# Four half-tile weight loads move from SyncE's DMA queue to ScalarE's, in a one-core attention and two-layer expert kernel

## The chip, the cores and the metric

The kernel runs on one core of a Trainium2 chip. The metric is the device time of one execution in microseconds (us). The time of a kernel is the median of several executions; one further execution was taken by the hardware profiler, and all rows below are from it. The engines are TensorE (PE, with its weight loads as PEld), VectorE (DVE), ScalarE (ACT), GpSimd (POOL) and SyncE (SP), which here only issues DMAs.

## The reference

The computation is a chunked attention followed by two gated feed-forward layers, in float32.

```python
# attention: 4 batches, 8 heads, 768 tokens, head size 64; chunks of 32 queries
# see 8 memory keys, 16 tokens to the left, the chunk, 8 tokens to the right
scores = scale * np.matmul(q_c, k_full.transpose(0, 1, 3, 2))
a = softmax(scores); out[:, :, c_start:c_end] = np.matmul(a, v_full)
# x: 3072 tokens x 512
h = x @ w_in                                    # 512 x 2048
x = h * (1.0 / (1.0 + np.exp(-1.702 * h))) @ w_out    # 2048 x 512
g = x @ w_gate; val = x @ w_val                 # 512 x 1536
y = g * (1.0 / (1.0 + np.exp(-g))) * val @ w_out      # 1536 x 512
```

The weights arrive as float64 words (the inputs that begin with `moe` are viewed as pairs of 32-bit words). The kernel turns each weight tile into float32 itself.

## The kernel before

The 3072 tokens are six blocks of 512, and each block is four groups of 128 tokens. Attention works on a group (g = 0 to 23): PE makes the scores (`scores_first`, L693), DVE subtracts the row maximum (L719, L720), ACT takes the exponential (L725), DVE and ACT sum, guard, invert and weigh (L736, L141, L144, L742), PE transposes the weights (L153), ACT copies them out of PSUM (`keep_e`, L162) and PE multiplies with the values (L169). For the first block ACT then rounds the attention output to the operand `xh` (`hi_x`, L757), keeps a copy (L764), DVE makes the remainder `xl` (L769), and PE starts the first feed-forward layer on `xh` and `xl` (`plain_up`, L542). Later blocks run in a steady order of products (L446) and down products (L581).

A weight tile comes from the array `wr` as 128 partitions of 512 eight-byte words, 512 KB. `load_raw` (L262) loads it into `raw`; three buffers rotate, and four spare tiles of the weight pool serve for tiles 3 to 6. A tile of `w_out` is one DMA (L271). A tile of `w_in` is reordered on the way: it is two DMAs of 256 KB (L276), one for partitions 0 to 63 (a = 0) and one for partitions 64 to 127 (a = 1), each of 256 pieces of 1 KB. Then ACT reads both halves in one instruction (`take_words`, L283), DVE shifts and joins the bits (L291, L296), ACT rounds to the high part of the weight (L250), and POOL or DVE makes the low part (L253).

The first tiles in load order are 0, 1, 4, 5, 2, 3, 6, 7 of `wr` (`AT`, L260); load positions 0 to 3 are all in-weights, so each is two halves.

The opening, up to some 57 us, is written out by hand as a list of names in `OPENING` (L951), and each engine runs its instructions in that order, SP's DMA issues among them. `ldw0` to `ldw3` are the loads of positions 0 to 3, `ldk`, `ldq`, `ldv` those of keys, queries and values of a group. On ACT's side, `ex` is the exponential, `ra` the guard, `pr` `take_words`, `ec` `keep_e`, `hi` `hi_x`, `wb`, `wv` and `wa` the high parts of weights, `xf` the copy. On DVE's side, `mx` is the maximum and its subtraction, `sm` the sum, `rc` and `wg` the inverse and the weighing, `cs` and `ct` the shift and the join. On PE's side, `sc`, `te`, `pv` and `ua` are scores, transposes, values and the first feed-forward products. The stretches of the list around the four loads are:

```python
z0 tb0 ldk0 ldq0 sc0 mx0 ex0 sm0 ra0 ldk1 ldk2 ldq1 ldq2 ldk3 sc1 ldk4 z2 z1 mx1 ex1 sm1 rc0 ldw0 ra1
sc2 mx2 ex2 ldq3 ldq4 wg0 pr0 cs0 sc3 sm2 ra2 rc2 wg2 ldv0 ldw1 ldv1 rc1 wg1 te0 ec0 pv0 te1 mx3 ex3 sm3
te2 pr1 ldv2 ec1 cs1 ct1 ldq5 wb0 ra3 rc3 wg3 ct0 ldv3 sumA0/G ec2 hi0 pv1 hi1 wbl0/G pv2 ldw2 ldw3 ldk5
ldk6 te3 xl0 ldq6 sumB0/G ldw4 wv0 xf0 sc4 hi2 xl2 ec3 wa0 wvl0/V pv3 wal0/G xf2 hi3 ua1 mx4 xl3 ldw5
ex4 ua0 ldv4 sm4 hiB0 loB0/G xl1 ra4 wg4 ...  hiA0 xf1 pr3 cs3 pr2
```

Between engines only true dependences make anyone wait. SP has one more kind of wait: a load waits until the load eight places before it has landed, since eight semaphores rotate over the DMAs.

Of the kernel before, what the change touches and what calls it, by code (L numbers as in the profile page):

```python
# [57 lines left out]
def tile_attention_moe_moe(  # L58
# [8 lines left out]
    nc = tc.nc  # L67
# [194 lines left out]
    def load_raw(upto):  # L262
        while len(raws) < min(upto, NRAW):
            i = len(raws)
            if RB <= i < RB + len(spare_raw):
                raws.append(spare_raw[i - RB])
            else:
                raws.append(rpool.tile([P, 512], I64, tag="raw", name="raw", bufs=RB))
            k = AT[i] if i < len(AT) else i
            if k >= 2 * NF1 or k % 4 > 1:  # L270
                nc.sync.dma_start(out=raws[-1], in_=wr[k])  # L271
                continue
            src = wr[k].rearrange("(e d) (b a n) -> a d b e n", e=2, b=2, a=2)
            for a in range(2):
                dst = raws[-1][64 * a : 64 * a + 64].rearrange("d (b e n) -> d b e n", b=2, e=2)
                nc.sync.dma_start(out=dst, in_=src[a])  # L276

    nraw, bits = [2 * len(AT)], {}

# [21 lines left out]
    def next_weights(out):  # L301

        i = nraw[0]
        load_raw(i + RB)
        nraw[0] += 1
        take_words(i)
        yield 0
        shift_words(i)
        yield 0
        join_words(i)  # L310
        out += [bits.pop(i), raws[i]]
# [557 lines left out]
    def tokens():  # L869
# [8 lines left out]
        "ldk": lambda g: load_kv_first("k", g),  # L878
        "ldv": lambda g: load_kv_first("v", g),
        "ldw": lambda i: load_raw(i + 1),  # L880
        "st": store_x,
        "sc": scores_first,
# [153 lines left out]
    for n, (ph, b, ua, ub) in enumerate(seq):  # L1036
# [6 lines left out]
        for u in range(ua, ub):  # L1043
# [47 lines left out]
            if u == ua and nxt is not None and not attends:  # L1091
                src = {1: xd, 2: yd}[nxt[0]][nxt[1]]
# [55 lines left out]
```

## Time and profile before

| what | value |
|---|---|
| median of 3 runs | 1184.48 us (1182.43 to 1184.59) |
| profiled execution | 1181.78 us, of which the span from first to last instruction is 1180.0 us |
| busy share of the span | PE 97%, PEld 88%, DVE 55%, ACT 48%, POOL 29% |
| DMA | 131.47 MB; mean 111 GB/s; in the first 29.5 us 287 GB/s |
| granted TensorE clock, mean | 0.999 |

Busy time says which engine works, not who holds up whom. The views that answer that are the chain of work that ended last, the list of waits, and the timeline of one engine. The span is 1180.0 us long, so one digit of the page's slices covers 29.5 us; the opening is about two of them. The time from a DMA's issue to its landing is given with each line that issues DMAs.

### The profile page before, as it was taken

What the parts mean: (1) busy time and instruction counts of PE and PEld (TensorE: products, weight loads), DVE (VectorE), ACT (ScalarE), POOL (GpSimd) and SP (SyncE); (2) the same over time, 40 slices, a digit from 0 to 9 for tenths busy, and PEclk for the clock granted to TensorE, in tenths of its full rate; (3) what the DMA queues carried; (4) which work ended last, traced back from release to release, by engine and by line L of the source; (5) the groups of instructions that cost most, each with busy time, mean ns of one, the idle gap of its engine ahead of it and who ended that gap; (6) DMA issues with size and microseconds to landing.
All of it is one profiled execution on the core that took longest, in us unless ns stands there. A gap on an engine that the chain in (4) does not pass through costs nothing.

```text
span 1180.0 us, 22292 instructions
## 1 busy us (share of the span) xinstructions
PE 1146.8 (97%) x8908; PEld 1036.3 (88%) x8908; DVE 651.1 (55%) x1130; ACT 567.9 (48%) x1185; POOL 340.5 (29%) x308
## 2 busy tenths in 40 slices
PE   4799999999999999999999999999999999999998
PEld 3688888888899989999998999999999999999997
DVE  5878756556755444443456555354465554454553
ACT  4876554555565445444355444343455543243342
POOL 2553240203534233221335432021245521021010
PEclk9999999999999999999999999999999999999999
DMA  9889835253362322421333321120225130330302
GB/s 287 269 224 269 202 110 166 86 161 92 107 188 81 126 81 81 143 90 36 120 113 116 99 91 51 58 72 1 97 94 169 36 108 2 107 99 10 108 26 83
DMA packets 62920, 131.47 MB, mean 111 GB/s; under 512 B 5728, under 2 KB 26208, under 8 KB 60512
## 3 DMA queue, kind: packets, MB, share of 16 engines
q1 hardware_dynamic: 62816, 130.05, 35.4%
q8 instruction: 70, 1.15, 0.4%
q14 instruction: 34, 0.28, 0.1%
HBM read 98.57 MB, written 31.46 MB: 110 GB/s over the span
## 4 chain that ended last, share of the span: by engine, by line
PE 89%; DVE 4%; ACT 3%; issue 2%; DMA 1%; POOL 1%; SPq 0%; DVEq 0%; ACTq 0%; POOLq 0%
PE y L581 37%; PE ps_a L446 27%; PE ps_c L446 12%; PE ps_b L446 9%; PE ps_s L196 1%; PE ps_o L169 1%; DMA xd<-xf 1%; PE ps_t L153 1%; PE ps_u L542 1%; PE ps_v L169 1%; DMA q<-in_qg 1%; DVE gs L561 0%; ACT g L547 0%; PE ps_k L706 0%; ACT b L428 0%
## 5 line engine op out<-in xcount | busy, mean ns | idle before, releaser
L446 PEld LDWEIGHTS ps_a<-b,w 128*128 128x128 f32 x2832 | 383.9, 189 | 36.9 <-DVE ps_a L498 4.2
L446 PE MATMUL ps_a<-b,w 128*128 128x256 f32 x2832 | 397.1, 283 | 3.5 <-DVE ps_a L498 2.1
L581 PE MATMUL y<-gs,w 128*128 128x512 f32 x1152 | 298.5, 395 | 2.9 <-DVE e L742 1.7
L581 PE MATMUL y<-w,gs 128*128 128x512 f32 x864 | 247.8, 395 | 0.6 <-DVE gs L561 0.5
L581 PEld LDWEIGHTS y<-gs,w 128*128 128x128 f32 x1152 | 204.2, 189 | 39.1 <-DVE gs L561 2.5
L446 PE MATMUL ps_c<-b,w 128*128 128x256 f32 x1224 | 179.1, 282 | 0.0
L446 PEld LDWEIGHTS ps_c<-b,w 128*128 128x128 f32 x1224 | 167.2, 190 | 8.8
L581 PEld LDWEIGHTS y<-w,gs 128*128 128x128 f32 x864 | 144.2, 190 | 14.4 <-DVE gs L561 1.8
L253 POOL TENSOR_TENSOR w<-wf,w 128x512 fp32r<-128x512 f32 (+1 forms) x66 | 75.9, 1151 | 221.5 <-ACT w L250 199.8
L446 PE MATMUL ps_b<-b,w 128*128 128x256 f32 x900 | 133.8, 285 | 0.4 <-DVE ps_b L483 0.3
L549 ACT ACTIVATE g<-ps_b 128x512 f32<-128x512 f32 x72 | 43.0, 598 | 166.2 <-DVE ps_b L504 166.2
L446 PEld LDWEIGHTS ps_b<-b,w 128*128 128x128 f32 x900 | 119.2, 192 | 3.9 <-issue 1.7
L432 DVE TENSOR_TENSOR b<-xl,b 128x512 fp32r<-128x512 f32 x72 | 64.4, 895 | 80.3 <-ACT b L428 80.1
L498 DVE TENSOR_TENSOR ps_a<-m,ps_a 128x256 f32<-128x256 f32 x115 | 48.9, 425 | 105.4 <-PE ps_a L446 99.2
L488 ACT COPY u<-ps_a 128x256 f32<-128x256 f32 x115 | 42.9, 373 | 106.4 <-PE ps_a L446 106.3
L411 POOL TENSOR_TENSOR xl<-xl,t 128x512 f32<-128x512 f32 x18 | 23.3, 1293 | 231.1 <-DVE t L408 229.8
L561 DVE TENSOR_TENSOR gs<-ps_a,gs 128x512 fp32r<-128x512 f32 x118 | 80.9, 685 | 11.8 <-ACT gs L557 11.5
L483 DVE TENSOR_TENSOR ps_b<-p,ps_b 128x256 f32<-128x256 f32 x115 | 49.2, 428 | 61.3 <-PE ps_b L446 56.7
L557 ACT CAST gs<-ps_a 128x512 fp32r<-128x512 f32 x118 | 69.8, 591 | 23.3 <-DVE ps_a L527 15.6
L527 DVE TENSOR_TENSOR ps_a<-g,ps_a 128x512 f32<-128x512 f32 x72 | 50.0, 694 | 45.7 <-PE ps_a L446 45.2
L504 DVE TENSOR_TENSOR ps_b<-u,ps_c 128x256 f32<-128x256 f32 x102 | 43.6, 427 | 50.1 <-PE ps_c L446 49.8
L479 ACT COPY p<-ps_a 128x256 f32<-128x256 f32 x115 | 43.0, 374 | 58.0 <-PE ps_a L446 54.0
(131 smaller groups left out, 1172.8 us busy)
## 6 DMA issues: line engine op xcount, KB each, us to landing
raw<-in_wr SPq DMA_DIRECT2D x49, 512.0 KB, 3.4
xl<-yd SPq DMA_DIRECT2D x12, 1024.0 KB, 4.8
vm<-in_vg SPq DMA_DIRECT2D x22, 512.0 KB, 4.6
kbd<-in_kg SPq DMA_DIRECT2D x32, 256.0 KB, 4.2
raw<-in_wr SPq DMA_DIRECT2D x30, 256.0 KB, 5.0
yp<-o SPq DMA_DIRECT2D x24, 256.0 KB, 3.0
xl<-xd SPq DMA_DIRECT2D x6, 1024.0 KB, 4.8
base<-yp SPq DMA_DIRECT2D x24, 256.0 KB, 3.4
```

Of the source, the lines that this page charges most:

```text
L253: eng.tensor_sub(w[:, 1, o : o + n], f, w[:, 0, o : o + n].bitcast(F32))
L432: (eng or self.engs[k]).tensor_sub(x[:, 1], self.source(k), x[:, 0].bitcast(F32))
L446: nc.tensor.matmul(ps, w[:, a, o + kc * P : o + kc * P + P], x[:, c, kc, :], start=(start and kc == 0 and (a, c) == PASSES[0]), stop=(kc = ...
L479: nc.scalar.copy(p1, ca[:, :n])
L483: add(cb[:, :n], p1, cb[:, :n])
L498: add(ca[:, n:], m, ca[:, :n])
L504: add(cb[:, n:], u2, cc)
L527: late[0] = [lambda: nc.vector.tensor_mul(ca, t, ca), lambda: gs.append(cast(ca))]
L549: nc.scalar.activation(t, c, AF.Silu)
L557: nc.scalar.copy(x[:, 0], g)
L561: nc.vector.tensor_sub(x[:, 1], g, x[:, 0].bitcast(F32))
L581: nc.tensor.matmul(y, lhs, rhs, start=(first and o == 0 and (a, c) == PASSES[0]), stop=(ends and o == len(gs) - 1 and (a, c) == passes[-1]),)
```

## The change

Of load positions 0 to 3, the half with a = 1 is issued by `nc.scalar.dma_start` in place of `nc.sync.dma_start`. Nothing else in the source differs. The names in `OPENING` stay where they are, so the issue comes on ACT's instruction stream at the place that `ldw0` to `ldw3` have in the list.

```diff
             for a in range(2):
                 dst = raws[-1][64 * a : 64 * a + 64].rearrange("d (b e n) -> d b e n", b=2, e=2)
-                nc.sync.dma_start(out=dst, in_=src[a])
+                (nc.scalar if a and i < 4 else nc.sync).dma_start(out=dst, in_=src[a])
```

## Rows read from the trace of the kernel before

**Rows 1.** The page: engines, the granted clock and GB/s in slices, the DMA queues.

```profile
PE 1146.8 (97%) x8908; PEld 1036.3 (88%) x8908; DVE 651.1 (55%) x1130; ACT 567.9 (48%) x1185; POOL 340.5 (29%) x308
...
q1 hardware_dynamic: 62816, 130.05, 35.4%
```

**Rows 2.** Chain that ended last, 0 to 60 us: start us, us, what.

```profile
16.08 0.44 DVE wf L291
...
31.35 4.37 PE ps_u L542 x18
...
37.07 2.69 issue
...
40.08 4.55 PE ps_u L542 x12
...
57.19 3.00 PE y L581 x12
```

**Rows 3.** ACT's timeline: start us, us, operation, output and input, [idle before, its releaser].

```profile
11.95 0.58 ACT L725 ACTIVATE ps_k<-ps_k 128x512 f32<-128x512 f32 x1 [2.39 <-DVE ps_k L720]
...
15.38 0.66 ACT L283 ACTIVATE wh<-raw 128x512 f32<-128x512 f32 x1
17.14 0.21 ACT L141 ACTIVATE r<-r 128x8 f32<-128x8 f32 x1 [1.09 <-DVE r L736]
18.75 1.18 ACT L162 COPY ebd<-ps_t 64x512 f32<-64x512 f32 x2 [1.40 <-PE ps_t L153]
20.58 0.58 ACT L725 ACTIVATE ps_k<-ps_k 128x512 f32<-128x512 f32 x1 [0.65 <-DVE ps_k L720]
21.83 0.68 ACT L283 ACTIVATE wh<-raw 128x512 f32<-128x512 f32 x1 [0.67 <-DMA raw<-in_wr]
23.04 1.18 ACT L162 COPY w<-ps_t 64x512 f32<-64x512 f32 x2 [0.53 <-PE ps_t L153]
...
30.92 0.65 ACT L757 CAST xh<-ps_v 128x256 fp32r<-128x256 f32 x2
...
34.14 0.67 ACT L283 ACTIVATE wh<-w 128x512 f32<-128x512 f32 x1
```

**Rows 4.** SP's timeline: half-tile issues in pairs, the sixth query load, the fifth value load.

```profile
4.82 1.65 SPq L276 DMA_DIRECT2D raw<-in_wr  x2
...
9.74 1.88 SPq L276 DMA_DIRECT2D raw<-in_wr  x2
...
15.37 0.33 SPq L669 DMA_DIRECT2D q<-in_qg  x1
...
28.98 0.33 SPq L689 DMA_DIRECT2D vm<-in_vg  x1
```

**Rows 5.** L276 alone, issues around 5 us, 11 us, 22 us, 25 us; then the whole run.

```profile
DMA to landing us min/median/max: 9.0/9.4/9.7
...
DMA to landing us min/median/max: 10.7/10.7/10.7
...
DMA to landing us min/median/max: 5.3/5.5/5.7
...
DMA to landing us min/median/max: 6.2/6.3/6.5
...
L276 SPq DMA_DIRECT2D raw<-in_wr x30: 595/616/1262, 4.8 to 346.3; - x30
...
DMA to landing us min/median/max: 3.5/5.1/10.7
```

**Rows 6.** PE's timeline: the scores of group 7.

```profile
49.57 0.86 PE L706 MATMUL ps_k<-w,qq 64*32 64x64 f32 x64
```

**Rows 7.** Stretches, PE alone: us, PE busy (x instructions), granted clock, DMA share, GB/s.

```profile
38.00:39.00 1.00, 0.00 (x0) 1.00 0.99 389
...
41.00:42.00 1.00, 1.00 (x4) 0.50 1.17 248
```

**Rows 8.** DMA queues between 37 and 38 us: packets, MB, share of 16 engines.

```profile
q8 instruction: 1, 0.02, 6.9%
```

## The prediction

> **What bounds the kernel now.** I read the page first, then the chain of waits, then the timelines of ACT and SP, and last the landing times of the one DMA line that changes. The page says PE is busy 97% of the span [rows 1], so from about 57 us on nothing but PE's own work matters, and what the opening loses or gains is handed on to the end one for one unless something with a time of its own absorbs it. The change touches only the opening, so the opening's chain is the thing to read. There the chain jumps between engines [rows 2]: it passes DVE's bit shift of the first weight tile at 16.08 and PE's first feed-forward products at 31.35; at 37.07 it has 2.69 us for which no releaser is seen; the first down product is at 57.19.
>
> Two of ACT's instructions stand exactly at the landing of a weight half. `pr0` (`take_words` of load 0) starts at 15.38 [rows 3]. Its second half was issued by SP as the later of the pair at 4.82, which spans 1.65 us [rows 4], so at about 5.6, and took 9.7 us to land [rows 5]: 15.3. And `pr1` starts at 21.83 with an idle time that the trace puts down to this DMA [rows 3]; its second half took 10.7 us [rows 5] from about 11.0 [rows 4], so it landed at 21.7. Both halves have no slack at all. And behind `pr1` ACT is the bound itself: from 23.04 its instructions stand back to back up to 31.57, the end of the last rounding (between the rows of 23.04 and 30.92 stand ten more, none with an idle time; the first and the last are shown) [rows 3], and PE's products follow it at once [rows 2].
>
> **What the change does.** Four issues leave SP and come on ACT. What they free on SP is 0.62 us each (616 ns is the median of the 30 such issues) [rows 5]; SP waits on landings and free buffers rather than on its own issue time, and nobody on the chain waits for SP here, so I cost that at zero. It would matter only for a load that stands on the chain: the fourth query load for `sc3` would land some 1.5 us earlier, but the transposes behind `sc3` must end in ACT's copy, which comes after `pr0` in ACT's order, so that gain is lost when `pr0` is late.
>
> What they get on ACT is a later place. ACT's order is ... `ex1`, second half of load 0, `ra1`, `ex2`, `pr0`, `ra2`, second half of load 1, `ec0`, `ex3`, `pr1`, `ec1`, `wb0`, `ra3`, `ec2`, `hi0`, `hi1`, second halves of loads 2 and 3, `wv0`, `xf0`, `hi2` ... An issue can't leave before ACT has come to it. Two unknowns have no row: how long a half takes from ACT's queue, since the trace shows only one queue of data DMAs, q1 [rows 1], and how long its issue holds ACT.
>
> For the landing, the near rows run from 3.5 us (the shortest of this line in the whole run) over 5.3 to 6.5 us (the four halves issued at 22 to 25 us, with several loads ahead of them) to 10.7 us (behind a full queue) [rows 5]. I take 5.3: a half on a queue of its own does not stand behind SP's backlog, yet shares the transfer with it. The Trainium skill, DMA: Bandwidth & Descriptors, section Queues, rings and completion order, says that each DMA engine goes round the queues that have work, packet by packet; by that the 10.7 us would not occur on ACT's queue. This trace, with one data queue, can't show it.
>
> For the issue I take the 0.62 us that it takes SP, fully exposed when ACT is busy, and zero as the other end (ACT's sequencer could issue while the instruction before still runs).
>
> **Step 1, load 0.** `ex1` ends at 11.95 + 0.58 = 12.53 [rows 3]. The half lands at 12.53 + 5.3 = 17.83, so `pr0` starts at about 17.85 rather than 15.38: 2.5 us late. The issue itself hides, as ACT is idle before `ra1`. Queued behind `pr0` are, on DVE, the shift (16.08 [rows 2]) and then the sum of group 2 that `ra2` waits for, and on ACT `ra2` and all that follows.
>
> **Step 2, load 1.** From the start of `pr0` to the end of `ra2` it is 17.35 - 15.38 = 1.97 us [rows 3], all in chain. So `ra2` ends at 19.82, the half is issued from there to 20.44, and lands at 19.82 + 5.3 = 25.1. `pr1` then starts at 25.1 rather than 21.83, 3.3 us late. It ends 0.68 later, at 25.8. `ec1`, at 23.04 before, had 0.53 us of idle time between, which absorbs that much: it starts at 25.8, 2.8 us late. The way over `ec0` is shorter: it starts at 20.44, 1.7 us late.
>
> **Step 3, loads 2 and 3.** They stand between `hi1` and `wv0`, in the stretch where ACT never idles: 2 x 0.62 = 1.24 us, which pass whole to `hi3` and to PE's products. They land in time: issued at about 30.0 and 30.6, with 6.5 us, the last is there at 37.1, and `pr3`, the first to read one, is at 34.14 before [rows 3] and so at about 38.2.
>
> **Step 4, SP's own waits.** Each load of SP waits for the one eight places before: the sixth query load went out at 15.37, when load 0's second half had landed at 15.3 [rows 4, 5]. So the late halves hold SP too: the fifth value load, out at 28.98 before [rows 4], comes to wait for the second half of load 2, to about 30.0 + 5.7 = 35.7 (5.7 is what that half took before [rows 5]). The first use of what comes behind it is at 49.57, the scores of group 7 [rows 6], so I cost that at nothing; if that cover is gone, it is a microsecond or two at the conversions of loads 6 and 7.
>
> **Sum.** 2.8 + 1.24 = 4.0 us later at PE's first feed-forward products, 35.4 rather than 31.35 [rows 2]. From there it is passed on. Against the profiled execution that is 1181.78 + 4.0 = 1185.8; the median of the runs shown is 2.7 above that execution, so for a median I say 1184.48 + 4.0 = 1188.5.
>
> **Bounds.** With 3.5 us of landing, `pr0` comes at 16.03 (0.65 late), `ra2` ends at 18.0, the half of load 1 lands at 21.5, and `pr1` must wait for `ex3` anyway, at 20.58 + 0.65 + 0.58 = 21.8: no delay. What is left is the issue on ACT, 0 to 1.24. With 10.7 us for load 0, `pr0` comes at 23.2 (7.85 late) and `ra2` ends at 25.2; by then SP's backlog has gone, so 5.3 for load 1: `pr1` at 30.5, 8.7 late, `ec1` 8.1 late, and with the issues 9.4.
>
> **Rivals.** *Nothing measurable.* ACT's queue is served quickly, at about 3.5 to 4.3 us, and the issues hide in part: 0 to 2.4 us, 1184.5 to 1186.9. For it speaks that a queue of its own needs no backlog; against it that the DMA engines are fully used at that time. The Trainium skill, the same page, section Rules for kernel authors, holds that spreading DMAs over issuing engines saves only issue time, and that two transfers to disjoint halves of the partitions share the same engines; by that the change would be worth nothing, 1184.5, which is this rival's lower end. No run here shows two queues yet.
>
> *A long landing.* 6.5 to 10.7 us, sum 6.5 to 9.4: 1191 to 1193.9. The rows of 9.0 to 10.7 at the same stretch [rows 5] speak for it; that those stood behind some eight loads of one queue speaks against.
>
> *Faster.* The 2.69 us at 37.07 in which PE waits for nothing that the profile shows lie in a stretch with the DMA share at 0.99, and one transfer of the instruction queue moved in it [rows 2, 7, 8]; PE then runs at a granted clock of 0.50 [rows 7], the lower level of 1.2 GHz, so that 12 feed-forward products take 4.55 us where 18 took 4.37 [rows 2]: 4.55 - 12 x 4.37 / 18 = 1.6 us more. If PE waits there for its instructions behind a full DMA, and SP's held loads (step 4) thin the traffic out, both go: -2.69 - 1.6 = -4.3. With a quick landing (+0.6, half the issue cost) that is -3.7: 1180.8. It decides below 2 us of net delay; with my sum of 4.0 it leaves about -0.3. Against it: SP's loads before are still in flight there, and each engine needs its fetch wherever it stands.
>
> *It doesn't do what it says.* If ACT's issue went out as early as SP's did, the sum is zero. It can't: ACT's stream is in order, and `ex1` waits for group 1's scores.
>
> **How the numbers follow.** A landing of 4.3 to 6.5 us, +2.4 to +6.5: 0.52. Long landing: 0.14. Nothing measurable, up to +2.4: 0.27. Faster: 0.07. About 0.2%, 2.4 us, is what a measurement of this kernel can tell from no change; so slower 0.66, same 0.27, faster 0.07. The range takes in the second and third case nearly whole, with half a microsecond for the spread of medians below: 1183.5 to 1193.0.
>
> **What would show it.** In the profile of after: `pr0` at 17 to 19 us with a wait put down to the DMA of `raw`; `pr1` at about 25; an issue of some 0.6 us on ACT's sequencer after `ex1`, `ra2` and `hi1`; PE's first products of L542 at about 35.4; a second data queue beside q1. I am wrong if `pr0` stays near 15.4, or if PE's first products of L542 are late and the first down product, at 57.19 before [rows 2], is not.

## The result, and the profile after

The changed kernel takes 1194.76 us (median of 4 executions, 1192.82 to 1195.48) against 1183.45 us for the kernel before (4 executions, 1181.32 to 1184.59). The ratio is 1.0095, with a 95% interval of 1.0074 to 1.0116: slower, by 11.3 us. The profiled executions are 1192.82 us against 1181.78 us, their spans 1191.0 against 1180.0. The forecast was slower by 4.0 us and a range up to 1193.0. The direction came true; the size did not, and the measured time lies above the range.

The page after has a second data queue, q10, which carries the four halves (1.05 MB). Its columns are packets, MB and the share of 16 engines' time:

```profile
q1 hardware_dynamic: 61728, 129.00, 34.7%
...
q10 hardware_dynamic: 1088, 1.05, 0.3%
```

The chain of work that ended last, in the first 60 us, its pieces longer than 4 us (start, duration, what). All four are landings of DMAs, three of them of in-weights; the 9.41 and the 12.27 are halves on ACT's queue:

```profile
4.66 9.25 DMA raw<-in_wr
...
13.93 9.41 DMA raw<-in_wr
...
34.01 12.27 DMA w<-in_wr
...
46.72 8.50 DMA q<-in_qg
```

ACT's timeline, the instructions of [rows 3] and, as ACTq, the four issues:

```profile
11.89 0.58 ACT L725 ACTIVATE ps_k<-ps_k 128x512 f32<-128x512 f32 x1 [2.28 <-DVE ps_k L720]
13.93 0.71 ACTq L276 DMA_DIRECT2D raw<-in_wr  x1
...
23.37 0.66 ACT L283 ACTIVATE wh<-raw 128x512 f32<-128x512 f32 x1 [7.99 <-DMA raw<-in_wr]
25.12 0.21 ACT L141 ACTIVATE r<-r 128x8 f32<-128x8 f32 x1 [1.09 <-DVE r L736]
25.12 0.60 ACTq L276 DMA_DIRECT2D raw<-in_wr  x1
25.77 1.18 ACT L162 COPY ebd<-ps_t 64x512 f32<-64x512 f32 x2 [0.44 <-issue]
28.56 0.58 ACT L725 ACTIVATE ps_k<-ps_k 128x512 f32<-128x512 f32 x1 [1.61 <-DVE ps_k L720]
29.17 0.67 ACT L283 ACTIVATE wh<-raw 128x512 f32<-128x512 f32 x1
30.06 1.18 ACT L162 COPY w<-ps_t 64x512 f32<-64x512 f32 x2 [0.22 <-PE ps_t L153]
...
33.37 0.60 ACTq L276 DMA_DIRECT2D raw<-in_wr  x1
33.55 0.67 ACT L757 CAST xh<-ps_v 128x256 fp32r<-128x256 f32 x2
34.01 0.63 ACTq L276 DMA_DIRECT2D w<-in_wr  x1
34.68 0.40 ACT L250 CAST w<-wf 128x256 fp32r<-128x256 f32 x1 [0.46 <-issue]
...
38.44 0.65 ACT L757 CAST xh<-ps_v 128x256 fp32r<-128x256 f32 x2
...
46.30 0.66 ACT L283 ACTIVATE wh<-w 128x512 f32<-128x512 f32 x1 [4.54 <-DMA w<-in_wr]
```

`pr0`, the first L283, waits 7.99 us for its half and starts 8.0 us late. `pr1` does not wait for a DMA at all: it follows `ex3` (L725 at 28.56). `pr3` waits 4.54 us. From issue to landing the four halves took 9.4, 3.5, 9.3 and 12.3 us.

PE's timeline shows what this does to the products (the lines in between are left out):

```profile
38.86 0.73 PE L542 MATMUL ps_u<-xh,a 128*128 128x512 f32 x2 [0.47 <-ACT xh L757]
...
48.10 0.33 PE L706 MATMUL ps_k<-w,qq 64*32 64x64 f32 x10 [3.47 <-issue]
49.47 3.44 PE L542 MATMUL ps_u<-xh,w 128*128 128x512 f32 x8 [1.04 <-ACT w L250]
...
67.11 3.01 PE L581 MATMUL y<-gs,w 128*128 128x512 f32 x12 [0.24 <-DVE e L742]
```

Against [rows 2] the first products are 7.5 us late (31.35 before), the second group 9.4 (40.08), the first down product 9.9 (57.19). The last load of tokens, issued at 1095.6 us before, is issued at 1106.1: 10.5 us late. So nearly all of the loss is made in the opening and carried to the end: 7.5 us up to the first products and 1.9 up to the second group. Of the 1.9 us, PE's wait for the rounding (L250) that comes behind `pr3` is 1.04; another 0.8 is a wait with no releaser, 3.47 us where it was 2.69 before [rows 2], and its cause isn't shown.

How a half moved on q10 is seen in the DMA queues per stretch. The first line is 14 to 18 us, the next two 18 to 19, the next two 19 to 20, the last one 26 to 27:

```profile
q1 hardware_dynamic: 588, 1.32, 105.5%
...
q1 hardware_dynamic: 106, 0.35, 98.4%
q10 hardware_dynamic: 11, 0.01, 3.2%
...
q1 hardware_dynamic: 77, 0.26, 78.3%
q10 hardware_dynamic: 78, 0.08, 25.1%
...
q10 hardware_dynamic: 42, 0.04, 19.3%
```

Load 0's half was issued at 13.93 and moved nothing before 18.8 us, while q1 moved 1.32 MB from 14 to 18 alone; then the two queues went packet for packet, 78 against 77, and as its packets are 1 KB and most of the others larger, it got 0.08 of 0.34 MB. Load 1's half, issued at 25.12 into an idle DMA, had its first packets at 26.5.

### The profile page after: what moved, and what is told of

Read it like the earlier page. It is cut to its first block, busy times and chain, and to the rows that moved or that the text cites. A ratio compares the mean times of both kernels' runs of the same rounds, so it can differ in the third digit from the quotient of the medians.

```text
span 1191.0 us, 22289 instructions
## 1 busy us (share of the span) xinstructions
PE 1149.9 (97%) x8908; PEld 1038.8 (87%) x8908; DVE 653.1 (55%) x1130; ACT 567.8 (48%) x1185; POOL 340.7 (29%) x308
## 3 DMA queue, kind: packets, MB, share of 16 engines
q10 hardware_dynamic: 1088, 1.05, 0.3%
## 4 chain that ended last, share of the span: by engine, by line
PE 88%; DMA 4%; ACT 3%; DVE 3%; issue 2%; POOL 1%; SPq 0%; DVEq 0%; ACTq 0%; POOLq 0%
PE y L581 37%; PE ps_a L446 27%; PE ps_c L446 12%; PE ps_b L446 9%; DMA raw<-in_wr 2%; PE ps_s L196 1%; PE ps_o L169 1%; DMA w<-in_wr 1%; PE ps_v L169 1%; DMA q<-in_qg 1%; PE ps_t L153 1%; ACT gs L557 0%; ACT b L428 0%; ACT ebd L162 0%; DVE gs L561 0%
## 5 line engine op out<-in xcount | busy, mean ns | idle before, releaser
L561 DVE TENSOR_TENSOR gs<-ps_a,gs 128x512 fp32r<-128x512 f32 x118 | 80.9, 686 | 11.8 <-ACT gs L557 11.5
```

The costliest lines, as they stand in the source:

```text
L561: nc.vector.tensor_sub(x[:, 1], g, x[:, 0].bitcast(F32))
```

## The experiments

Theory P: what costs is the place. A half that is issued at ACT's place comes late and stands behind what SP has already issued; the cost counts where its reader is on the chain. Rival Q: the second queue itself costs, per half that is moved. Later a third question is added: whether it is ACT's queue or the backlog that makes the landing long.

The first four share a set of runs of the kernel before (11 executions, 1182.79 us), the next four another (19 executions, 1183.39 us), and the last has its own (7 executions, 1183.41 us).

### Load 0 alone

```diff
-                (nc.scalar if a and i < 4 else nc.sync).dma_start(out=dst, in_=src[a])
+                (nc.scalar if a and i == 0 else nc.sync).dma_start(out=dst, in_=src[a])
```

> Only load 0 has its second half on ACT's queue. Theory P (place and landing): the half goes out at 12.5 to 14 us on ACT and lands some 9 us later behind what SP has issued; pr0 starts at 22 to 23.5 us, 7 to 8 us late; pr1 then waits for nothing, ec1 is 7 to 8 us late, and the whole is 7 to 8.5 us longer than before. Rival Q (the second queue itself costs, per half that is moved): a quarter of the whole loss, 2.5 to 3 us.

Measured: 1192.4 us, ratio 1.0075 (1.0060 to 1.0090), 9.6 us longer. ACT's timeline:

```profile
15.97 0.70 ACTq L276 DMA_DIRECT2D raw<-in_wr  x1
26.36 0.66 ACT L283 ACTIVATE wh<-raw 128x512 f32<-128x512 f32 x1 [8.95 <-DMA raw<-in_wr]
...
32.16 0.67 ACT L283 ACTIVATE wh<-raw 128x512 f32<-128x512 f32 x1
32.73 1.17 ACT L162 COPY w<-ps_t 64x512 f32<-64x512 f32 x2
```

`pr0` is 11.0 us late and `ec1` 9.7; the landing took 10.3 us. That is P, and even more than P expected, since the issue went out only at 15.97. ACT had come to it at about 12.6, the start of `ex1` in this run. The chain of this run tells what it waited for: the fourth query load, issued by SP at 5.75, whose 10.20 us end at that moment.

```profile
5.75 10.20 DMA qq<-in_qg
15.97 10.31 DMA raw<-in_wr
```

The fourth query load stands eight places before the half when the DMAs of both engines are counted in the order in which they go out. So the eight rotating semaphores hold ACT too. In the changed kernel it was load 0's first half, landed at 13.91, that let ACT issue at 13.93.

### Load 1 alone

```diff
+                (nc.scalar if a and i == 1 else nc.sync).dma_start(out=dst, in_=src[a])
```

> Only load 1 has its second half on ACT's queue. P: pr0 stays at 15.4 us; the half goes out at 17.3 us, behind ra2, and lands after 8 to 9.5 us, so pr1 starts at 25.5 to 27 us, 3.7 to 5 us late; ec1 0.5 us less; the whole 3 to 4.5 us longer. Q: 2.5 to 3 us longer, with pr1 near 22 us.

Measured: 1188.13 us, ratio 1.0039 (1.0026 to 1.0053), 5.3 us longer, more than either number (P's was 3 to 4.5); `pr1`, at 26.71, is where P had it. The half went out at 18.61 and took 8.1 us:

```profile
18.61 0.71 ACTq L276 DMA_DIRECT2D raw<-in_wr  x1
...
26.71 0.66 ACT L283 ACTIVATE wh<-raw 128x512 f32<-128x512 f32 x1 [4.08 <-DMA raw<-in_wr]
27.27 1.17 ACT L162 COPY w<-ps_t 64x512 f32<-64x512 f32 x2
```

`pr1` is 4.9 us late and `ec1` 4.2. Part of it, 1.5 us, was there at `pr0` already (16.85, waiting 0.97 us for its half on SP): the second query load, issued at 2.60, took 6.99 us in this run where it had taken 6.46. The moved half went out long after that, so this part isn't its doing, and why that load took longer is open.

### Loads 2 and 3 alone

```diff
+                (nc.scalar if a and i in (2, 3) else nc.sync).dma_start(out=dst, in_=src[a])
```

> Only loads 2 and 3 have their second halves on ACT's queue. P: nothing moves before 26 us; the issues hold ACT 0.5 to 1.2 us between hi1 and wv0; the halves land 9 to 12 us after issue, at 37 to 40 us, so pr3 (34.1 us before) waits until then, and PE's products behind its weight (40.0 us before) start at 42 to 43.5 us; the whole 2 to 4 us longer. Q: two halves, 5 to 6 us longer.

Measured: 1187.5 us, ratio 1.0039 (1.0024 to 1.0054), 4.7 us longer, between the two numbers. The landing is as P says: ACT's timeline has nothing moved by more than 0.6 us up to 23 us, and then

```profile
26.61 1.59 ACTq L276 DMA_DIRECT2D w<-in_wr  x1
...
39.93 0.66 ACT L283 ACTIVATE wh<-w 128x512 f32<-128x512 f32 x1 [4.24 <-DMA w<-in_wr]
```

The chain gives this half 13.30 us from the start of its issue, so `pr3` is 5.8 us late, and the products behind its weight start at 43.11, 3.0 us late. PE's timeline, and two stretches (us, PE busy, granted clock, DMA share, GB/s), show that `pr3`'s wait is the smaller part of this:

```profile
32.80 1.22 PE L542 MATMUL ps_u<-xh,a 128*128 128x512 f32 x2 [0.47 <-ACT xh L757]
...
43.11 3.78 PE L542 MATMUL ps_u<-xh,w 128*128 128x512 f32 x8 [0.63 <-ACT w L250]
...
33.00:34.00 1.00, 1.00 (x3) 0.50 1.04 328
...
47.00:48.00 1.00, 1.00 (x4) 0.50 1.04 287
```

The first products were 1.45 us late already, behind the two issues on ACT (0.72 us idle after them) and what follows. PE waits only 0.63 us for the rounding behind `pr3`. And PE runs parts of both groups at a granted clock of 0.50, the lower level of 1.2 GHz, where before it ran the first at 1.00 and the second at 0.50 for a shorter time: the first 18 products and the next 12 take 5.31 and 5.49 us against 4.37 and 4.55 [rows 2]. These pieces add up to the 4.0 us by which the first down product (61.17) is late. Before the clock fell, PE had stood idle for 1.89 us up to 30.80 (1.17 before, in both cases for ACT's copy) and for 2.51 us up to 42.03 (2.69 before); what set it off was not tried, and P did not have it.

### All four on ACT's queue, issued earlier

The four second halves get names of their own in `OPENING`, so that they stand where ACT is idle: load 0's behind the first table load, load 1's before `ex1`, those of loads 2 and 3 behind `ra2`. The first halves stay in SP's order.

```diff
-z0 tb0 ldk0 ldq0 sc0 mx0 ex0 sm0 ra0 ldk1 ldk2 ldq1 ldq2 ldk3 sc1 ldk4 z2 z1 mx1 ex1 sm1 rc0 ldw0 ra1
+z0 tb0 ldk0 ldq0 ldk1 ldk2 ldq1 ldq2 ldk3 ldk4 ldw0 lg0/S lh0/A sc0 mx0 ex0 sm0 ra0 sc1 z2 z1 mx1 ldq3 ldq4 ldv0 ldw1 lg1/S lh1/A ex1 sm1 rc0 ra1
-sc2 mx2 ex2 ldq3 ldq4 wg0 pr0 cs0 sc3 sm2 ra2 rc2 wg2 ldv0 ldw1 ldv1 rc1 ...
+sc2 mx2 ex2 wg0 pr0 cs0 sc3 sm2 ra2 ldw2 ldw3 lh2/A lh3/A rc2 wg2 ldv1 rc1 ...
```

> All four second halves on ACT's queue as in the change, but each issue stands earlier in ACT's order: load 0's behind the first table load, load 1's ahead of ex1, those of loads 2 and 3 behind ra2; the first halves stay in SP's order where they were. P: the halves are there when they are read; pr0 at 15 to 16.5 us, pr1 at 21 to 23 us; the whole within 1.5 us of before (0.6 us may be lost where load 0's half shares the transfer with the second query load, which is on the chain). Q: as long as the changed kernel, 8 to 12 us longer.

Measured: 1186.87 us, ratio 1.0028 (1.0016 to 1.0041), 4.1 us longer. This is far from the 11.3 of the changed kernel, so Q falls; but it misses P's 1.5 us, and `pr0` (17.67) and `pr1` (23.50) miss their windows. No reader waits for a half here. More than half of the loss is made at the second query load, which the early half delays:

```profile
2.60 8.86 DMA q<-in_qg
```

It took 6.46 us before, so 2.4 us of the loss are there at 11.46 us, where I had allowed 0.6. Load 0's half, issued at 2.18, moved its packets from 6.8 us on, packet for packet with SP's queue (87 against 90 between 7 and 8 us).

### Load 0's half late, on SP's own queue

```diff
-... rc0 ldw0 ra1 sc2 mx2 ex2 ldq3 ldq4 wg0 pr0 ... wg2 ldv0 ldw1 ldv1 rc1 ... te2 pr1 ldv2 ec1
+... rc0 ldw0 lg0/S ra1 sc2 mx2 ex2 ldq3 ldq4 ldv0 ldw1 ldv1 ldv2 lh0/S wg0 pr0 ... wg2 rc1 ... te2 pr1 ec1
```

> Nothing on ACT's queue. The second half of load 0 alone is moved, in SP's own order, from behind its first half to behind the third value load, so that SP issues it at about 13 us, the time at which the changed kernel has it go out on ACT. Theory P (the late place behind the queued loads costs, whichever queue issues it): it lands 9 to 11.5 us later, pr0 starts at 22 to 25 us and the whole is 7 to 10 us longer than before, as in e1_first. Rival Q (ACT's queue is what is slow): it lands in 5 to 6 us like SP's halves of 22 us, pr0 at 18 to 19 us, and the whole is 2 to 4 us longer.

Measured: 1191.52 us, ratio 1.0070 (1.0055 to 1.0085), 8.1 us longer. SP issued the half at 13.70, and it took 11.8 us:

```profile
13.70 0.61 SPq L880 DMA_DIRECT2D raw<-in_wr  x1
...
25.52 0.66 ACT L283 ACTIVATE wh<-raw 128x512 f32<-128x512 f32 x1 [10.18 <-DMA raw<-in_wr]
```

So without any second queue the late place costs nearly the same. ACT's queue is not slower than SP's at that time: 9.4 us (changed kernel) and 10.3 (load 0 alone) against 11.8.

### Less traffic around the half

Load 0 alone on ACT's queue again, but SP's loads of load 1 and of the values of groups 0 to 2 are left out and those buffers are set to zero by POOL; the output is therefore not the reference's.

```diff
-z0 tb0 ldk0 ...          wg2 ldv0 ldw1 ldv1 rc1 ...  te2 pr1 ldv2 ec1
+z0 tb0 zv0 zv1 zv2 ldk0 ...  wg2 zw1 rc1 ...         te2 pr1 ec1
```

> As e1_first (second half of load 0 on ACT's queue at the place of the change), but SP's loads of load 1 and of the values of groups 0 to 2 are left out, and POOL sets those buffers to zero, so the output is not the reference's; 2 MB less stand ahead of or beside the half. Theory B (the half stands behind what SP has already issued): issued at 11.9 to 14 us, its first packet moves at most 3 us later and it lands in 3.5 to 6 us rather than 10.3; pr0 at 16 to 19.5 us. Rival: ACT's queue is slow by itself, first packet 4 to 5 us after the issue and landing after 8 us or more, pr0 after 20.5 us.

Measured in one execution (1185.8 us, not compared, since the work is not the same): the half is issued at 12.14, its first packets move at 14.6 us, and it lands after 6.2 us rather than 10.3:

```profile
12.12 0.58 ACT L725 ACTIVATE ps_k<-ps_k 128x512 f32<-128x512 f32 x1 [2.45 <-DVE ps_k L720]
12.14 0.71 ACTq L276 DMA_DIRECT2D raw<-in_wr  x1
...
18.46 0.66 ACT L283 ACTIVATE wh<-raw 128x512 f32<-128x512 f32 x1 [2.94 <-DMA raw<-in_wr]
```

The landing is 0.2 us above the bound expected, the rest as theory B said: it is the backlog that makes the landing long, and here the issue also left at once, 0.02 us after `ex1` began, as the eighth load before it had landed.

### Three halves early, load 0 as before

```diff
-z0 tb0 ldk0 ldq0 sc0 mx0 ex0 sm0 ra0 ldk1 ldk2 ldq1 ldq2 ldk3 sc1 ldk4 z2 z1 mx1 ex1 sm1 rc0 ldw0 ra1
+z0 tb0 ldk0 ldq0 sc0 mx0 ex0 ldk1 ldk2 ldq1 ldq2 ldk3 ldk4 ldw0 ldq3 ldq4 ldv0 ldw1 lg1/S lh1/A sm0 ra0 sc1 z2 z1 mx1 ex1 sm1 rc0 ra1
-... ra2 rc2 wg2 ldv0 ldw1 ldv1 rc1
+... ra2 ldw2 ldw3 lh2/A lh3/A rc2 wg2 ldv1 rc1
```

> Load 0 stays on SP as before; the second halves of loads 1, 2 and 3 are on ACT's queue, load 1's issued behind ex0 and those of loads 2 and 3 behind ra2. P: each lands before its reader; pr0 at 15 to 16 us, pr1 at 21 to 22.5 us, PE's first products of L542 at 31 to 32.5 us; the whole within 1 us of before. Q (a cost per half on the second queue): 5 to 8 us longer.

Measured: 1185.16 us, ratio 1.0011 (1.0000 to 1.0022), 1.8 us longer. P's 1 us is missed by 0.8, and Q's 5 to 8 is far off. `pr0` is at 16.30 and `pr1` at 22.27, and PE's first products at 32.95, 1.6 us late; the first and the last are 0.3 and half a microsecond outside P's windows. The three halves cost no more than these 1.8 us. ACT's issue had to wait until 11.61 here, and `ex1` behind it started at 12.56 (11.95 before), 0.6 of the 1.6 us.

### SP's order alone

```diff
-... ldk1 ldk2 ldq1 ldq2 ldk3 sc1 ldk4 z2 ...   ldv0 ldw1 ldv1 rc1
+... ldk1 ldq1 ldk2 ldq2 ldk3 sc1 z2 ...        ldv0 ldw1 ldk4 ldv1 rc1
```

> No queue is changed: in SP's order the second query load goes ahead of the third key load, and the fifth key load goes behind load 1. If the landing of what SP issues is the limit of the opening up to pr1, as P says, then 0.5 MB less stands ahead of the second query load (9.06 us before), of load 0 and of load 1: sc1 at 7.8 to 8.2 us, pr0 at 14 to 14.5, pr1 at 20.4 to 20.9, and the whole 0.7 to 1.5 us shorter than before. If the opening is limited by the engines instead, nothing changes (within 0.5 us).

Measured: 1182.93 us, ratio 0.9999 (0.9989 to 1.0010): no change, so the number missed. The first steps came as expected: `sc1` at 8.03, `pr0` at 14.28, PE's first products at 30.35, 1.0 us early. `pr1`, at 21.36, waited 1.31 us for its half and missed its window. By PE's second group the gain was gone:

```profile
40.38 0.45 PE L706 MATMUL ps_k<-w,qq 64*32 64x64 f32 x10 [3.29 <-issue]
40.76 3.36 PE L542 MATMUL ps_u<-xh,w 128*128 128x512 f32 x8
```

It starts 0.7 us later than before (40.08 in [rows 2]), behind a wait of 3.29 us for nothing that the profile shows, which was 2.69 us before. What PE waits for there was not tried.

### The change without load 0

```diff
-                (nc.scalar if a and i < 4 else nc.sync).dma_start(out=dst, in_=src[a])
+                (nc.scalar if a and 1 <= i < 4 else nc.sync).dma_start(out=dst, in_=src[a])
```

> The change without its load 0: loads 1, 2 and 3 have their second halves on ACT's queue at the places of the change. P: pr0 at 15.4 to 17 us; load 1's half lands 8 to 9.5 us after an issue at 17.4 to 18.7, so pr1 at 26 to 28 us and ec1 3 to 5 us late; the halves of loads 2 and 3 land 9 to 12 us after an issue at about 31, so pr3 waits to 40 to 43 us; the whole 5 to 7 us longer than before, some 4 to 6 us less than the changed kernel loses. If load 0 is not the main part, it is as long as the changed kernel, 9 to 11 us.

Measured: 1191.72 us, ratio 1.0072 (1.0045 to 1.0099), 8.3 us longer, above the 5 to 7 expected. The losses of parts do not add: load 0 alone 9.6, the other three together 8.3, all four 11.3. The trace says why. Here load 1's half took 8.1 us and `pr1` waited 4.14 us for it; in the changed kernel the same half took 3.5 us and nobody waited, since `pr0` was so late that SP, whose next value load waits for group 0's products, had run dry. And the pair:

```profile
31.27 0.63 ACTq L276 DMA_DIRECT2D w<-in_wr  x1
...
44.05 0.66 ACT L283 ACTIVATE wh<-w 128x512 f32<-128x512 f32 x1 [4.77 <-DMA w<-in_wr]
```

It took 12.8 us and `pr3` waited 4.77, as in the changed kernel (4.54). So that second wait is there whether or not load 0 is moved. What it costs PE is 1.03 us here, as in the changed kernel (1.04):

```profile
45.76 0.44 PE L706 MATMUL ps_k<-w,qq 64*32 64x64 f32 x10 [3.62 <-issue]
47.23 3.78 PE L542 MATMUL ps_u<-xh,w 128*128 128x512 f32 x8 [1.03 <-ACT w L250]
```

The wait without a releaser before it is longer than before in both kernels too (3.62 and 3.47 against 2.69), and whether the late halves have a part in that was not tried. The time of load 0 alone can't be subtracted from that of the whole change to price this, because the issue of load 0's half waited 2 us longer there (15.97 against 13.93).

## Why the prediction was right in direction and wrong in size

- **What bounds the opening** held for a loss. `pr0` waits for its moved half, and `pr1` does so in the runs of load 1 alone and without load 0, and the delay is carried to the end: 9.9 us at the first down product, 10.5 us at the last load of tokens, 11.0 in the spans. The last microsecond is within the spread of the executions and is not explained further. A gain was not carried on: SP's order alone brought PE's first products 1.0 us earlier and the end not at all.
- **SP's freed issues at zero** held as far as shown: SP's loads went out up to 3.0 us earlier (the second value load at 9.69 against 12.71, the sixth query load at 12.94 against 15.37 in [rows 4]) and no reader on the chain gained.
- **Step 1 failed, in two terms.** The first is a wait that I left out. I had the eight rotating semaphores hold SP's loads (step 4) but not ACT's issues: the half left at 13.93 rather than 12.53, 1.4 us later, because ACT waited for load 0's first half (in the run of load 0 alone it came to the issue at 12.6 and waited 3.4 us for the fourth query load). The second is the landing, 9.4 us where I took 5.3: 4.1 us. Together 5.5 us, and `pr0` came at 23.37 rather than 17.85. The row that I chose was the wrong one: 5.3 to 6.5 us was measured where SP had just restarted (its issue before was at 15.37, the next at 22.00), and the row of the same stretch, 9.0 to 10.7 us [rows 5], was the nearer. I put it aside because a queue of its own would not stand behind SP's backlog. It does, for a while: in the loaded cases (13.93; in the runs of load 0, load 1 and the pair alone 15.97, 18.61 and 25.84; without load 0 18.59 and 30.61) the first packet came 3.3 to 5.6 us after the issue, 4.9 in the changed kernel, against 1.4 us into the idle DMA at 25.12; after that it shared packet for packet. How the backlog holds the first packet, no run shows. By the Trainium skill, DMA: Bandwidth & Descriptors, section Queues, rings and completion order, the engines go round the queues packet by packet; the trace agrees from the first packet on (78 against 77 of the profile's packets between 19 and 20 us), and the wait before the first packet is not in that rule.
- **Step 2** had the way from `pr0` to the end of `ra2` right (23.37 to 25.33, 1.96 us against 1.97) and load 1's landing wrong the other way: 3.5 us, as the DMA had emptied meanwhile. So this half cost nothing, and `ec1` is 7.0 us late from load 0 alone, through `ex3` and PE.
- **Step 3's issues** were sized at 1.24 us and cost 0.46 us of ACT's time: the first ran from 33.37 to 33.97, beside the L757 of `hi0` and `hi1`. **Step 3's landings** failed: 9.3 and 12.3 us instead of 6.5, so `pr3`, which I had given 1.1 us to spare, waited 4.54 us, and PE waited 1.04 us for the rounding behind it. With 0.8 us more of the wait without a releaser, PE's second group lost 1.9 us more.
- **Step 4** came out near nothing, as said. The late halves do hold SP (the fifth value load at 35.23 instead of 28.98), and the chain names one of the held loads, the query load of 8.50 us issued at 46.72, which SP reaches only when load 3's half has landed. But the copy (L162) that the chain puts behind it follows ACT's L141 at 0.11 us, where it was 0.10 before, so no wait is seen there. At most it is part of the 0.5 us between the second group (9.4 us late) and the first down product (9.9).
- **The bounds.** The long landing, 6.5 to 9.4 us, was the rival that came true, at a chance of 0.14. Its upper end has `pr0` at 23.2, and 23.37 was measured, in part by luck: the landing there is 10.7 us and was 9.41, and the wait of the issue is missing. It has 9.4 us at PE's first products, where 7.5 was measured, since load 1's half cost nothing; what it lacks is all that came behind the first products, 3.5 us in the spans. One sum is off by itself: a landing of 4.3 us, by the prediction's own steps, gives `pr1` at 23.1, `ec1` at 23.8 and 2.0 us in all, not 2.4. Of the faster rival the traces show nothing: PE's wait without a releaser is in every run, 2.5 to 3.6 us at the scores of group 6.
- **The rule on spreading DMAs** (the Trainium skill, the same page, section Rules for kernel authors, holds that it saves only issue time): the runs agree in that none gained from the second queue. That the change would then be worth nothing was the prediction's conclusion; the nearest to it is 1.8 us, with three halves issued early, and at the place of this change it was 11.3.

## What to carry to other kernels

A DMA that moves to an in-order compute engine's queue is issued when that engine comes to it, so look for how early it went out before and what was queued by then, not for the time that the issue itself takes. Price its landing by the row of the same stretch, at the depth of queue that will be there, and take a second queue as a share of the same transfer rather than as a way past it. And follow every semaphore that rotates over all queues: a wait for an earlier transfer that was harmless on the DMA-only engine stops the compute engine.

## What the runs showed of the hardware that was not expected

- A half on a second queue waited 3.3 to 5.6 us for its first packet while the first queue was full, 2.5 us with less traffic, and 1.4 us when it was empty (25.12 to 26.5 us); 1.32 MB of the first queue passed in 4 us of the wait at 13.93.
- When both had work, they alternated by packet, so the queue with 1 KB packets got about a quarter of the bytes beside larger ones (0.08 of 0.34 MB in a microsecond).
- An issue on ACT took 0.60 to 0.74 us, once 1.59 (the second of the pair alone), but it can run beside an activation: two in a busy stretch left ACT idle for 0.46 us in the changed kernel and 0.72 us for the pair alone.
- A 256 KB half put early on a second queue, in front of a query load of 256 KB on the first, made that load land 2.4 us later, after 8.86 us instead of 6.46.
